# A fixed order of operations, and transposes by quarters, in a kernel of a recurrence and an MLP on one core

## The chip, the cores and the metric

One core of one Trainium2 chip. The time is the device time of one execution in microseconds (us); the span of a profile is some 1.7 us shorter than the time of its run. The engines are PE (TensorE; PEld is its weight load), DVE (VectorE), ACT (ScalarE), POOL (GpSimd) and SP (SyncE, which here only issues DMAs).

## The reference

```python
# r, k, v, w, a, b: 4 x 8 heads x 768 steps x 40, float32
for t in range(768):
    y[:, :, t] = einsum('bhd,bhde->bhe', rt, state)
    Sa = einsum('bhde,bhe->bhd', state, at)
    state = state * wt[:, :, None, :] - einsum('bhd,bhe->bhde', Sa, bt) \
          + einsum('bhd,bhe->bhde', vt, kt)
x = y as 3072 tokens x 320
g = softplus(x @ w_in)            # 320 -> 2048
out = g @ w_out                   # 2048 -> 320
```

The kernel does the recurrence in 12 chunks of 64 steps. For each pair of chunks ("window") it has to invert triangular blocks; the first two of the six inversions run on DVE and the last four on POOL. Around each chunk stand some 40 small groups of matmuls, among them six transposes of 128x1024 tiles (k, v, r, a, n, u), 72 in all.

## The kernel before

Every operation is an object with its reads, writes and engine. A greedy scheduler orders them at build time. It holds a model in which PE's instructions arrive in blocks of 256, and keeps slow operations (h, o, csb) for the places where a block ends. The constants are the model's own; the traces below show the 256, no run tests the others:

```python
BLOCK, AHEAD, FETCH, BEFORE = 256, 82, 2300.0, 70
SLOW = ("h", "o", "csb")
FILL, SAVE, MARGIN = 10826.01, 385707354.55, 0

class Fetch:
    def run(self, start, cost, n, keep=False):      # n: PE instructions of the operation
        ...                                         # cut: walks over the block borders
            if at == edge:
                w = max(0.0, asked + FETCH - t)     # the next block isn't there yet
                stall += w
                t += w
...
                if e == "pe":
                    pen += fetch.run(s + pen, c, 2 * COUNT[o.name])
                    if o.name in SLOW:
                        want = FILL if fetch.wants(s) else -SAVE
```

A transpose is 8 products over the whole array:

```python
        def transpose(src, srcs, t, off):
            def f(e):
                for bp in X2:
                    for yy in range(H_ // 2):
                        i = T.transpose(pb(t)[:, bp, off + 128 * yy:off + 128 * yy + 128],
                                        src[:, bp, 128 * yy:128 * yy + 128], ident[:, :])
                return i
            return op(pe(8 * 56.0), srcs + ["ident"], [t], f, mode=FULL, name="tr")
```

Line numbers in views of this kernel: L664 input loads, L705 sum over wout, L730 transposes, L773 grams, L967 and L971 POOL's inversion, L960 the transpose into mt that starts an inversion, L976 the mb product that ends it, L1205 and L1224 the two products of the MLP.

Of the kernel before, what the change touches and what calls it, by code (L numbers as in the profile page):

```python
# [15 lines left out]
L = 64  # L16
# [6 lines left out]
FIRST = ["v3", "b1", "v0", "w2", "k3", "b3", "b2", "r1", "k2", "v2", "r2", "b0", "a3", "v1", "a0", "a2", "k1", "k0",  # L23
    "w0", "a1", "r0", "r3"]
BY_ACT = ("a2", "b0", "k0h", "k3h", "r1h", "r2", "r2h", "v1", "w0",)
# [3 lines left out]
DUE = {}  # L29
TUNED = {("const", 0): (-3.417, 6.015), ("logs", 0): (8.233, 4724148.243), ("logs", 2): (6.841, 0.057),  # L30
    ("logs", 4): (27.193, 37726.657), ("logs", 6): (2.37, 391.709), ("logs", 8): (14.554, 0.031),
    ("logs", 10): (8.533, 0.075), ("first", 0): (-7.498, 4.706), ("first", 1): (-5.316, 0.851),
    ("first", 2): (7.047, 0.321), ("first", 3): (12.848, 2139.634), ("first", 4): (-17.941, 0.029),
    ("first", 5): (-5.232, 3.903), ("first", 6): (-2.842, 1.343), ("first", 7): (-9.63, 0.459),
    ("first", 8): (-0.391, 1.153), ("first", 9): (-12.18, 0.032), ("first", 10): (-3.891, 0.348),
    ("first", 11): (-5.631, 0.071), ("invert", 0): (-22.825, 124.863), ("invert", 1): (-5.682, 0.826),
    ("invert", 2): (-8.703, 0.205), ("invert", 3): (-3.704, 1.381), ("invert", 4): (-11.375, 1974.653),
    ("invert", 5): (-15.966, 18675.296), ("weights", 0): (11.186, 0.069), ("csb", 0): (19.338, 0.424),
    ("before", 0): (-9.639, 3.123), ("before", 1): (-0.307, 0.833), ("before", 2): (-7.054, 0.041),
    ("before", 3): (3.482, 0.394), ("before", 4): (-2.541, 0.33), ("before", 5): (-1.866, 0.119),  # L40
    ("before", 6): (-7.662, 6.411), ("before", 7): (7.568, 1.936), ("before", 8): (-2.958, 0.61),
    ("before", 9): (5.556, 0.241), ("before", 10): (3.509, 267110.005), ("before", 11): (-3.86, 15.709),
    ("W", 0): (14.734, 23.158), ("W", 1): (0.519, 1.563), ("W", 2): (2.341, 16.473),
    ("W", 3): (-3.294, 0.056), ("W", 4): (-1.178, 0.263), ("W", 5): (13.312, 49401.102),
    ("W", 6): (-3.378, 0.377), ("W", 7): (18.075, 0.091), ("W", 8): (6.58, 0.055), ("W", 9): (-16.669, 0.712),
    ("W", 10): (9.283, 52.11), ("W", 11): (5.588, 5.518), ("chain", 0): (-1.124, 0.658),
    ("chain", 1): (-1.317, 6.807), ("chain", 2): (-0.072, 0.086), ("chain", 3): (0.801, 0.66),
    ("chain", 4): (-0.995, 0.105), ("chain", 5): (-1.411, 10.836), ("chain", 6): (4.897, 11.085),
    ("chain", 7): (6.353, 307.324), ("chain", 8): (6.613, 11.615), ("chain", 9): (-7.081, 16.525),
    ("chain", 10): (0.443, 0.025), ("chain", 11): (-4.429, 7146.58), ("after", 0): (-0.303, 0.423),  # L50
    ("after", 1): (-8.387, 1.433), ("after", 2): (-1.682, 0.269), ("after", 3): (-16.392, 0.075),
    ("after", 4): (-13.518, 0.174), ("after", 5): (-11.687, 4.319), ("after", 6): (-6.304, 14.814),
    ("after", 7): (-11.267, 7.2), ("after", 8): (13.486, 10.526), ("after", 9): (0.785, 0.169),
    ("after", 10): (-1.398, 0.029), ("after", 11): (-8.768, 0.036), ("mlp", 0): (-8.041, 4.047),
    ("mlp", 1): (-5.331, 0.069), ("mlp", 2): (-5.684, 0.09), ("mlp", 3): (-6.455, 0.429),
    ("mlp", 4): (-9.333, 0.438), ("mlp", 5): (-15.828, 2.29), ("mlp", 6): (-18.549, 0.02),
    ("mlp", 7): (-5.284, 0.029), ("mlp", 8): (-11.139, 8.71), ("mlp", 9): (5.482, 16.833),
    ("mlp", 10): (-13.205, 18.475), ("mlp", 11): (-5.182, 0.355), ("load w", 4): (-6.939, 16.423),
    ("load w", 6): (-2.291, 0.065), ("load w", 8): (-4.5, 2.09), ("load w", 10): (-8.097, 83.127),
    ("load a", 4): (-1.093, 7.381), ("load a", 5): (12.999, 232.282), ("load a", 6): (-5.685, 150.299),  # L60
    ("load a", 7): (-6.287, 0.467), ("load a", 8): (8.128, 0.02), ("load a", 9): (21.502, 0.203),
    ("load a", 10): (-13.753, 0.788), ("load a", 11): (19.743, 62.662), ("load b", 4): (-5.978, 3.007),
    ("load b", 5): (-6.732, 26.773), ("load b", 6): (-15.345, 42671.34), ("load b", 7): (-9.402, 930.573),
    ("load b", 8): (-18.389, 1513.939), ("load b", 9): (-10.847, 80.591), ("load b", 10): (-14.935, 372.451),
    ("load b", 11): (-16.972, 2570.875), ("load k", 4): (-3.826, 10.505), ("load k", 5): (-15.524, 5807.389),
    ("load k", 6): (-6.188, 192.352), ("load k", 7): (-17.635, 719690.433), ("load k", 8): (-15.96, 2784.456),
    ("load k", 9): (-1.453, 375.087), ("load k", 10): (-22.642, 248.71), ("load k", 11): (-9.44, 14.74),
    ("load v", 4): (-10.722, 8957201.34), ("load v", 5): (5.402, 75.257), ("load v", 6): (11.64, 137128.864),
    ("load v", 7): (3.577, 7946.204), ("load v", 8): (1.82, 1286492.642), ("load v", 9): (11.637, 0.83),
    ("load v", 10): (-0.375, 23529.721), ("load v", 11): (0.874, 18043.764),  # L70
    ("load r", 4): (-12.216, 481.059), ("load r", 5): (-0.558, 0.561), ("load r", 6): (-2.182, 0.845),
    ("load r", 7): (-9.889, 580669.095), ("load r", 8): (-8.828, 15940.927),
    ("load r", 9): (-5.276, 1095633.975), ("load r", 10): (13.622, 714172.543), ("load r", 11): (5.476, 0.162)}
# [27 lines left out]
class Op:  # L101
    def __init__(self, engines, reads, writes, fn, mode=None, dma=None, name="", fence=None):
        self.engines = engines
        self.fence = fence
        self.fn = fn
        self.mode = mode
        self.dma = dma
        self.name = name
        self.preds = set()
        self.tiles = list(dict.fromkeys(t for t in map(tile_of, list(reads) + list(writes)) if t))  # L110
        self.tail = 0.0
        self.eng = None
        self.start = self.end = self.seen = 0.0


class Graph:


    def __init__(self):
        self.ops = []  # L120
        self.res = {}
        self.streams = {}
        self.tag = ""
        self.stage = (0.0, 0.0)
        self.stages = {}
        self.chunk = {}

    def op(self, engines, reads, writes, fn, mode=None, dma=None, name="", fence=None):
        o = Op(engines, reads, writes, fn, mode, dma, name, fence)
# [29 lines left out]
        self.stages.setdefault(self.tag, (self.stage, []))[1].append(o)  # L159
        return o  # L160

    def deadlines(self):

        for (due, length), ops in self.stages.values():
            for i, o in enumerate(ops):
                o.due = due + length * (i + 0.5) / len(ops)


LAT = {"pe": 240.0, "dve": 130.0, "act": 150.0, "pool": 130.0, "sp": 0.0}
SELF = 75.0  # L170
SWITCH = 150.0
PEN = 311.61
PERIOD = 25000.0
BETA = 0.67


BLOCK, AHEAD, FETCH, BEFORE = 256, 82, 2300.0, 70

PORT = ("scale", "fw")
SLOW = ("h", "o", "csb")  # L180
FILL, SAVE, MARGIN = 10826.01, 385707354.55, 0
COUNT = {"tr": 8, "tot": 16, "gram": 32, "cum": 8, "W": 32, "X1": 16, "X": 32, "D": 32, "U": 32,
         "S1": 4, "S": 64, "sT": 32, "y1": 16, "y": 64, "yT": 6, "h": 6, "o": 4, "csb": 16}


class Fetch:
    def __init__(self):
        self.at = BEFORE
        self.asked = 0.0
        self.total = 0.0  # L190

    def run(self, start, cost, n, keep=False):

        at, asked, left, t = self.at, self.asked, n, start
        stall = 0.0
        each = cost / n
        while left:
            edge = (at // BLOCK + 1) * BLOCK
            step = min(left, edge - at)
            ask = edge - AHEAD  # L200
            if at < ask <= at + step:
                asked = t + each * (ask - at)
            t += each * step
            at += step
            left -= step
            if at == edge:
                w = max(0.0, asked + FETCH - t)
                stall += w
                t += w
        if keep:  # L210
            self.at, self.asked = at, asked
            self.total += stall
        return stall
# [39 lines left out]
def schedule(ops):  # L253
# [18 lines left out]
    while ready:  # L272
        cands = []
        for o in ready:
# [22 lines left out]
            if not ok:  # L297
                continue
# [1004 lines left out]
```

## Time and profile before

The time is 348.28 us (348.22 to 350.63, 3 runs). The prediction below shows the page's busy shares and three stretches: A, to the third transpose into mt (112.7 us); B, the four inversions on POOL (181.6 us); C, the rest (51.5 us).

### The profile page before, as it was taken

To read this page: it belongs to the slowest core of one execution; us is meant where nothing else is said; L and a number is where in the kernel's file an instruction comes from. 1 tells how busy PE (TensorE), PEld (TensorE's weight loads), DVE (VectorE), ACT (ScalarE), POOL (GpSimd) and SP (SyncE) were. 2 spreads that over 40 slices of the span, in tenths; PEclk is the share of its full clock that TensorE was granted. 3 is DMA by queue.
4 is the path that set the end of the run, shared out by engine and by line. 5 is a ranking of instruction groups with operands and counts; after the bars stand their busy time and mean duration, and the time that the engine had idled before them with its cause. 6 is when DMAs were issued, how large, how long until landed. Compare 5 with 4: busy or idle time off the path is not lost.

```text
span 345.8 us, 17638 instructions
## 1 busy us (share of the span) xinstructions
PE 280.4 (81%) x8016; PEld 212.7 (61%) x8016; DVE 232.7 (67%) x419; ACT 210.3 (61%) x296; POOL 169.2 (49%) x309
## 2 busy tenths in 40 slices
PE   0337247688789969999799999998989899999873
PEld 0226126576567747777577776786766678777642
DVE  7729978889997746657756697585885656664201
ACT  1246704226797825877568888667687368667661
POOL 8106000001000627898888788898888888000000
PEclk9967865569999978999899999999999999999999
DMA  8999984687667565676546465430411400100101
GB/s 134 171 174 142 182 159 79 107 145 113 122 120 156 103 112 94 123 126 108 102 79 104 83 104 96 78 69 14 89 34 21 91 14 13 33 6 21 39 22 38
DMA packets 145787, 31.30 MB, mean 90 GB/s; under 512 B 140272, under 2 KB 145392, under 8 KB 145712
## 3 DMA queue, kind: packets, MB, share of 16 engines
q1 hardware_dynamic: 129504, 25.09, 42.9%
q10 hardware_dynamic: 13728, 2.46, 5.1%
q0 software_dynamic: 2480, 2.62, 4.7%
q8 instruction: 63, 1.03, 1.2%
q14 instruction: 12, 0.10, 0.1%
HBM read 28.84 MB, written 3.93 MB: 95 GB/s over the span
## 4 chain that ended last, share of the span: by engine, by line
PE 47%; ACT 11%; POOL 9%; DMA 9%; SPq 9%; DVE 7%; issue 5%; ACTq 2%; DVEq 0%; POOLq 0%
PE ps L1205 12%; PE ps L1224 12%; SPq L664 8%; PE ps L730 7%; POOL mt L971 4%; DMA wout<-in_moe_w_out_dram 3%; POOL mtmp L967 3%; ACT gT L1214 3%; ACT et L1211 3%; PE ps L773 2%; DMA a_f<-in_a_dram 2%; PE ps L1073 2%; ACTq L664 2%; DMA r_f<-in_r_dram 2%; PE ps L1174 2%
## 5 line engine op out<-in xcount | busy, mean ns | idle before, releaser
L1205 PE MATMUL ps<-xT,win 128*128 128x256 bf16 x576 | 79.9, 275 | 3.5 <-ACT et L1211 1.8
L1211 ACT ACTIVATE et<-ps 128x512 f32<-128x512 f32 x96 | 57.2, 596 | 36.3 <-PE ps L1205 35.8
L967 POOL TENSOR_TENSOR mtmp<-mt 128x30 f32<-128x30 f32 (+14 forms) x120 | 60.5, 504 | 33.0 <-DVE mt L960 24.3
L971 POOL TENSOR_TENSOR mt<-mt,mtmp 128x30 f32<-128x30 f32 (+14 forms) x120 | 66.8, 557 | 8.7
L1224 PE MATMUL ps<-wout,gT 128*128 128x320 bf16 x384 | 65.2, 302 | 5.9 <-ACT gT L1214 2.9
L1205 PEld LDWEIGHTS ps<-xT,win 128*128 128x128 bf16 x576 | 50.6, 98 | 15.9 <-ACT et L1211 6.0
L1214 ACT ACTIVATE gT<-et,hln 128x1024 bf16<-128x1024 f32 x48 | 55.2, 1151 | 1.4
L1224 PEld LDWEIGHTS ps<-wout,gT 128*128 128x128 bf16 x384 | 34.2, 98 | 20.1 <-ACT gT L1214 4.6
L1035 POOL CAST r_b<-r_f 128x640 bf16<-128x640 f32 x12 | 9.5, 789 | 44.2 <-DMA r_f<-in_r_dram 39.6
L1035 POOL CAST v_b<-v_f 128x640 bf16<-128x640 f32 x12 | 9.2, 765 | 37.0 <-DMA v_f<-in_v_dram 24.8
L1229 DVE TENSOR_TENSOR osb<-ps,csb 128x320 f32<-128x320 f32 x24 | 11.6, 484 | 20.3 <-PE ps L1224 20.1
L785 DVE TENSOR_TENSOR qt<-ps,sut 128x1024 bf16<-128x1024 f32 x12 | 14.6, 1221 | 5.6 <-PE ps L773 5.6
L814 PE MATMUL ps<-lw,nexc 64*64 64x320 bf16 x96 | 7.2, 361 | 13.8 <-ACT lw L845 13.6
L814 PE MATMUL ps<-lw,ninc 64*64 64x320 bf16 x96 | 9.8, 328 | 8.5 <-ACT ginv L862 6.2
L785 DVE TENSOR_TENSOR tak<-ps,sut 128x1024 bf16<-128x1024 f32 x12 | 14.6, 1219 | 2.8 <-PE ps L773 2.6
L785 DVE TENSOR_TENSOR pt<-ps,sut 128x1024 bf16<-128x1024 f32 x12 | 14.6, 1216 | 2.6 <-PE ps L773 2.6
L1180 DVE TENSOR_TENSOR yo<-ps,gexc 128x640 bf16<-128x640 f32 x12 | 9.9, 821 | 8.3 <-PE ps L1174 8.2
L845 ACT ACTIVATE lw<-w_f 128x1280 bf16<-128x1280 f32 x6 | 7.7, 1282 | 12.3 <-DMA w_f<-in_w_dram 12.3
L868 DVE TENSOR_TENSOR kh<-k_f,ginv 128x640 bf16<-128x640 f32 x12 | 10.9, 910 | 4.8 <-DMA k_f<-in_k_dram 4.8
L985 ACT ACTIVATE dex<-dc,blk 128x1024 bf16<-128x1024 bf16 x6 | 6.9, 1146 | 11.6 <-DVE dc L979 11.6
L866 DVE SCALAR_TENSOR_TENSOR nh<-b_f,ginv 128x640 bf16<-128x640 f32 x12 | 9.9, 825 | 5.3 <-ACT ginv L862 5.3
L862 ACT ACTIVATE ginv<-ps 128x640 f32<-128x640 f32 x12 | 8.4, 704 | 8.0 <-issue 6.8
(152 smaller groups left out, 587.9 us busy)
## 6 DMA issues: line engine op xcount, KB each, us to landing
out_dram<-osb SPq DMA_DIRECT2D x48, 80.0 KB, 2.3
b_f<-in_b_dram SPq DMA_DIRECT2D x44, 80.0 KB, 3.6
v_f<-in_v_dram SPq DMA_DIRECT2D x44, 80.0 KB, 3.3
a_f<-in_a_dram SPq DMA_DIRECT2D x44, 80.0 KB, 3.4
k_f<-in_k_dram SPq DMA_DIRECT2D x44, 80.0 KB, 3.6
r_f<-in_r_dram SPq DMA_DIRECT2D x42, 80.0 KB, 3.1
w_f<-in_w_dram SPq DMA_DIRECT2D x20, 160.0 KB, 4.2
wout<-in_moe_w_out_dram POOLq DMA_DIRECT2D x4, 320.0 KB, 10.0
```

The lines of the kernel that those rows point to most:

```text
L664: lambda e, bp=bp, x=x, q=q: queue(e).dma_start(heads(t[q:q + 64, bp, :], D_), SRC[n][2 * bp + x][:, c * L:(c + 1) * L, :].rearrange("h p ...
L730: i = T.transpose(pb(t)[:, bp, off + 128 * yy:off + 128 * yy + 128], src[:, bp, 128 * yy:128 * yy + 128], ident[:, :])
L785: lambda e: V.tensor_tensor(parity(dst), bh(pf(t), L), bc4(mask[:, :], L), ALU.mult), name="mask")
L814: i = T.matmul(pf(t)[s:s + 64, bp, 0:DM], mats[z][q:q + 64, :], heads(lwt[q:q + 64, bp, :], 2 * D_)[:, :, z * D_:z * D_ + D_], start=(z == ...
L967: lambda e, j=j, nt=nt, tv=tv: E_.tensor_tensor(tv, m[:, 0:j, j:j + 1].to_broadcast([128, j, nt]), m[:, j:j + 1, j + 1:32].to_broadcast([1 ...
L971: lambda e, j=j, tv=tv: E_.tensor_tensor(m[:, 0:j, j + 1:32], m[:, 0:j, j + 1:32], tv, ALU.add),
L1035: lambda e, dst=dst, src=src: P.tensor_copy(hd(dst), bh(src, D_)), name="cast")
L1205: i = T.matmul(one(t)[:, 256 * (q % 2):256 * (q % 2) + 256], win[:, z, q * 128:(q + 1) * 128], xT_[:, z, :], start=(z == 0), stop=(z == 2))
L1211: lambda e, q2=q2, t=t, ett=ett: A.activation(ett[:, q2 % 2, :], one(t), AF.Exp), name="exp")
L1214: lambda e, q2=q2, ett=ett: A.activation(gts[q2 // 2][0][:, :, :].rearrange("p q m -> p (q m)"), ett[:, :, :].rearrange("p q m -> p (q m)" ...
L1224: i = T.matmul(one(t)[:, 0:DM], gts[z][0][:, q % 4, bp * 128:(bp + 1) * 128], wout[:, q, :], start=(q == 0), stop=(q == NQ - 1))
L1229: lambda e, t=t, ot=ot: V.tensor_tensor(ot[:], one(t)[:, 0:DM], csb[:], ALU.add), name="oe")
```

## The change

The intent: an order of all 1,839 operations, drawn up ahead by a local search, replaces the scheduler, and with it the scheduler's model of blocks. ACT may issue every input load, and does issue 61 of them (26 before). Of the 72 transposes 55 go by 64x64 quarters, 32 products in place of 8. Some operations change their engine as well (by the pages ACT has 284 instructions in place of 296, POOL 318 in place of 309). The work is otherwise the same. The core of the diff:

```diff
-BLOCK, AHEAD, FETCH, BEFORE = 256, 82, 2300.0, 70
-class Fetch:
-    ...
-def schedule(ops):
-    ...
+ORDER = (105, 86, 0, 97, 64, 103, ...)        # 1,839 numbers
+ENGINE = ("ggggvvvv...")                      # an engine for each
+BANK = ("4244426664...")                      # a PSUM bank for each tile
+QUARTERS = (
+    "111011110111100111111110110111111011101110011111111110011110110111010110")
+def arrange(ops):
+    ...                                       # hands out banks, returns
+    return [ops[n] for n in ORDER]
 ...
-                        i = T.transpose(pb(t)[:, bp, off + 128 * yy:off + 128 * yy + 128],
-                                        src[:, bp, 128 * yy:128 * yy + 128], ident[:, :])
+                        n = off + 64 * (4 * bp + yy)
+                        for q in (0, 64) if mode == QUAD else ():
+                            for o in (0, 64):
+                                i = T.transpose(pb(t)[o:o + 64, q // 64, n:n + 64],
+                                                src[q:q + 64, bp, 128 * yy + o:128 * yy + o + 64], eye(q))
+                        if mode == FULL:
+                            i = T.transpose(...)          # as before
 ...
-                    op(issuers(n, c, bp), [], [nm + "%d%d" % (bp, x)],
+                    op({"sp": 680.0, "act": 680.0}, [], [nm + "%d%d" % (bp, x)],
 ...
-        g.deadlines()
-        order = schedule(g.ops)
+        order = arrange(g.ops)
```

Line numbers in views of the changed kernel: L560 loads, L629 transposes by quarters, L632 whole ones, L601 sum over wout, L722 running sums, L875 and L879 POOL's inversion, L868 transpose into mt, L1115 and L1134 the MLP.

## The prediction

> **What bounds the kernel now.** I read the page first (busy shares, then the slices), because a kernel with five engines at 49 to 81% has no single bound and one must see when each engine is full.
>
> ```profile
> PE 280.4 (81%) x8016; PEld 212.7 (61%) x8016; DVE 232.7 (67%) x419; ACT 210.3 (61%) x296; POOL 169.2 (49%) x309
> ...
> DVE  7729978889997746657756697585885656664201
> ...
> POOL 8106000001000627898888788898888888000000
> ```
>
> The DVE digits are 7 to 9 in the first third and fall afterwards; POOL is nearly empty up to slice 13, then 8 to 9 without a break up to slice 34, then nothing. So there are three stretches. The tile view of mt gives the two borders: the third transpose into mt (the start of the first inversion that POOL does) begins at 112.65 us, and the last mb product of POOL ends at 294.3. Busy times in these windows (columns: window, its length, then busy us and count for PE, PEld, DVE, ACT, POOL, then clock, DMA share, GB/s):
>
> ```profile
> 0.00:112.70 112.70, 69.62 (x1984) 52.21 (x1985) 91.66 (x213) 55.01 (x77) 18.88 (x45) 0.82 0.88 139
> 112.70:294.30 181.60, 168.20 (x5090) 129.78 (x5088) 122.68 (x177) 125.85 (x178) 150.28 (x264) 0.97 0.45 79
> 294.30:345.80 51.50, 42.59 (x947) 30.70 (x945) 18.36 (x30) 29.44 (x43) 0.05 (x1) 0.99 0.12 26
> ```
>
> Stretch A (112.7 us): DVE is busy 91.7, idle 21.0. DVE sets it, with the loads behind it (DMA share 0.88). Stretch B (181.6): POOL runs four inversions one after another, 264 instructions, busy 150.3; PE is busy 168.2. Both are close to the bound. Stretch C (51.5): the last two chunks and their MLP, PE 42.6.
> Next the waits and the timelines, for what the stretches lose:
>
> ```profile
> PE ps L705 <- DMA wout<-in_moe_w_out_dram: 5.6, 1, 5.6
> ...
> ACT ginv L862 <- issue: 6.8, 1, 6.8
> ...
> DVE nh L866 <- ACT ginv L862: 5.3, 1, 5.3
> ```
> ```profile
> 130.98 0.72 POOL L1035 CAST v_b<-v_f 128x640 bf16<-128x640 f32 x1 [7.49 <-DMA v_f<-in_v_dram]
> ```
>
> The ACT timeline shows what "issue" is: ACT is issuing six DMAs from 14.4 to 21.8 while ginv is due, and DVE waits behind it. In the chain from 112 to 126 there is nothing but SP issuing one load after another at 0.64 us each; v lands last, and POOL stands 7.5 us in the middle of its inversion.
>
> [...] These lines of the PE timeline (start, duration) let one read the rate from start to start:
>
> ```profile
> 182.47 0.61 PE L730 MATMUL ps<-ident,kh 128*128 128x128 bf16 x8
> 182.92 0.61 PE L730 MATMUL ps<-ident,v_b 128*128 128x128 bf16 x8
> 183.37 0.71 PE L1224 MATMUL ps<-wout,gT 128*128 128x320 bf16 x4
> ...
> 185.70 0.45 PE L773 MATMUL ps<-aT,kT 40*64 40x64 bf16 x32
> 185.98 0.45 PE L814 MATMUL ps<-lw,ninc 64*64 64x320 bf16 x4
> ...
> 189.39 0.61 PE L730 MATMUL ps<-ident,nh 128*128 128x128 bf16 x8
> 189.93 0.47 PE L814 MATMUL ps<-lw,nexc 64*64 64x320 bf16 x8
> ```
>
> A transpose by 8 whole blocks takes 0.45 us (182.47 to 182.92 to 183.37); 0.54 when a quarter-array operation follows (189.39 to 189.93). L1205 shows the same: 0.66 before a full-array operation, 0.76 before a quarter one. So a switch costs 0.10 us. Thirty-two 64x64 products on four quarters take 0.28 us (185.70 to 185.98).
> [...] 0.45/8 is 56 ns, [...] 0.28/32 is 8.8 ns, with four tiles at work.
> [...] The page has 63 packets of 1.03 MB on the instruction queue, and 16,032 PE instructions are 62.6 blocks. [...] PEld's idle time ended by "issue" adds up to some 20 us.
> [...] One queue at 0.64 us per 80 KB gives at most 125 GB/s, while the first slices reach 171 to 182. So here issue time matters.
>
> **The change, part by part.** I compared the order of instructions in the two built programs; no arithmetic is added or taken away, 8,016 matmuls become 9,336 only because 55 of 72 transposes now go by 32 quarters instead of 8 blocks.
> - Quarters: 55 x (0.45 - 0.28) = 9.4 us less PE work. That a 64x64 transpose runs as fast as a 64x64 product has a witness in the kernel before: L926 transposes dex by 32 such quarters, and the next group starts 0.28 us after it (96.29 to 96.57 in the PE timeline).
> - Mode switches: 243 before, 185 after; 58 x 0.10 = 5.8 us. Together 15 us of 251 us warm PE work (each kind of group by its start-to-start time, summed).
> - Cost: 2,640 more PE instructions, 10 more code blocks. At 20 us for 63 blocks that is 3 us if they are placed no better than now.
> - Loads: ACT issues 61 input loads instead of 26, SP 203 instead of 238, in another order. The weight loads stay with POOL. ACT's first exponents now stand before most of its issues, w goes first on both queues, and the sum over wout (L705, which held PE 5.6 us) moves from PE row 22 to row 40, behind the inversion products.
> - Order: before the third transpose into mt, DVE has 201 instructions instead of 213. Less: two rT, one vT, one aT copies (0.69 each), xb 0.44, dex 0.54, two osb 0.49, omask 0.64, eight memsets of about 0.2, in all 7.0. More: kT 0.69, kh 0.82, yb 0.44, two tlo 0.6, in all 3.2. So DVE work is 91.7 - 3.8 = 87.9. Both DVE inversions are interleaved now, so each fills the other's waits.
>
> Stretch A: 87.9 of DVE plus idle. Of the 21.0 us idle I take off the 5.3 behind ginv, 1.4 behind the wout sum, and 1 of the start: 13 left, A = 101.
> Stretch B: POOL has the same 264 instructions. 181.6 less the 7.5 wait is 174. PE has to do 159.5 us of warm work between the same two borders in the new order (158.7 in the old, where it took 181.6). That fits, but barely; I add 1: B = 175.
> Stretch C: 37.1 us of PE work after the last inversion against 40.0, by the same sums, so 3 less, and 2 less waiting: C = 46.5. The very end stays: the last MLP goes exp, ln, last products, sum, store, and ACT sets it.
> Sum 322.5 of span. The time is 1.8 (profiled run) to 2.5 us (medians) above the span: **324.5 us**, say 324. The parts on the path are A -12, B -7, C -5; the 15 us of PE work are mostly not a gain of their own in A and B, they are what allows DVE and POOL to run without waiting.
>
> **Rivals.**
> - POOL stays the bound and nothing before it moves: if the new A is no shorter, because DMA (share 0.88 in A) is the true limit, only B and C gain: 336. For it: 141 input loads stand before the third mt transpose, against 138. Against it: many of these aren't needed by then.
> - PE takes B over: with fetch stalls in runs of quarter operations (18,672 instructions, in B also 93% full) B ends at 180 instead of 175. Then 330.
> - ACT becomes the loser: 35 more issues of about 0.66 us are 23 us of ACT time, on top of 210 busy. ACT waited 36 us for L1205 alone, so there is room, but a DMA issue that stands before an exp or a copy on the chain delays the chain. It would cost some us in A; 328 to 332.
> - The search did better than I think: A near 95 (DVE 92% full), no waits in B, C at 43: 314.
> - The order was drawn up for durations that the chip doesn't keep; a fixed order then waits in place where it could have gone on. Since the old order was fixed at build time as well, this is no new weakness; I give it little.
>
> **Range and chances.** The rivals lie at 314 to 336 and I see none above 341.3 (2% faster) except two of them at once, or a new stall that the order cannot show. Range 313 to 336; faster 0.93, within 2% 0.05, slower 0.02.
>
> **What would show it.** Windows with the new borders: third mt transpose at 96 to 107, last mb end 173 to 178 later, rest 43 to 50. PE timeline: quarter transposes 0.28 us start to start. PE busy about 265. POOL without a wait above 3 us for v. The wait of L705 for wout gone, or off the chain. The prediction is wrong if the third mt transpose comes at 110 or later, if POOL stands waiting between inversions, or if the quarters take as long as the whole transposes (32 at over 14 ns) or "issue" before PE and PEld grows by over 8 us.

## More of the kernel before

```profile
q8 instruction: 63, 1.03, 1.2%
...
PE 47%; ACT 11%; POOL 9%; DMA 9%; SPq 9%; DVE 7%; issue 5%; ACTq 2%; DVEq 0%; POOLq 0%
...
POOL mtmp L967 <- DVE mt L960: 24.3, 1, 24.3
```

The reader is to see that 63 packets of instructions come, a number that looks harmless beside 1.2%; that POOL is part of the chain; and that POOL waits for mt once, before its first inversion, and never between two of them.

## The result, and the profile after

The changed kernel takes **366.92 us** (364.8 to 368.9, 4 runs), the kernel before in the same rounds 348.71 (348.22 to 350.63). The ratio is 1.0511, 95% interval 1.0439 to 1.0582: slower. A ratio is the mean time of one kernel's fast runs over that of the other's fast runs of the same rounds, so it isn't quite the ratio of the medians. Executions over 1.5% slower than the fastest of the same kernel are left out of the means.

The page after, busy times first, then the instruction queue and the chain:

```profile
PE 283.2 (78%) x9336; PEld 210.9 (58%) x9336; DVE 236.2 (65%) x422; ACT 200.9 (55%) x284; POOL 170.5 (47%) x318
...
q8 instruction: 73, 1.20, 1.3%
...
PE 56%; DVE 16%; SPq 8%; issue 7%; ACT 6%; DMA 5%; ACTq 0%; DVEq 0%
```

PE's busy time, which I expected near 265, has not fallen, POOL has left the chain, and PE's share of it has grown. The granted clock isn't what made it slower: its mean was 0.948 in this run and 0.924 in that of the kernel before. The three stretches with the same borders (window, length, then busy us and count of PE, PEld, DVE, ACT, POOL, then clock, DMA share, GB/s):

```profile
0.00:120.20 120.20, 65.94 (x2377) 49.83 (x2378) 86.40 (x200) 54.98 (x72) 20.84 (x53) 0.90 0.81 131
120.20:312.20 192.00, 172.84 (x5964) 129.56 (x5965) 128.82 (x187) 117.39 (x171) 148.89 (x264) 0.97 0.40 74
312.20:365.10 52.90, 44.38 (x1010) 31.55 (x998) 20.94 (x35) 28.58 (x41) 0.75 (x2) 1.00 0.13 29
```

A is 7.5 us longer, B 10.4, C 1.4. In B POOL does the same 264 instructions in about the same 149 us, but now it waits itself. The list of waits (engine line waited for: us in total, times, longest):

```profile
POOL mtmp L875 <- DVE mt L868: 17.9, 4, 9.0
PEld ps L629 <- issue: 16.7, 15, 5.3
...
PE ps L629 <- issue: 3.8, 5, 1.3
...
PEld ps L981 <- issue: 3.8, 15, 0.5
```

POOL waits four times for mt, so three times between inversions, which the prediction named as a sign of being wrong. And PE stands at "issue", that is, for nothing that the profile shows: all such waits sum to 16.3 us before products (4.1 in the kernel before) and 46.9 before weight loads (20.7). The PE timeline shows how they look (start, duration, in brackets the idle time and what ended it):

```profile
92.80 1.46 PE L1115 MATMUL ps<-xT,win 128*128 128x256 bf16 x6
94.19 0.64 PE L629 MATMUL ps<-ident,ah 64*64 64x64 bf16 x32
94.64 0.24 PE L629 MATMUL ps<-ident,kh 64*64 64x64 bf16 x3
96.02 0.59 PE L629 MATMUL ps<-ident,kh 64*64 64x64 bf16 x29 [1.14 <-issue]
```

One transpose of 32 products stops after its third product for 1.14 us and goes on. No operand changes there, no semaphore is asked. Counting PE's instructions in the built program (a product is two, its weight load and itself; a second wait is one more) puts this stop, and the others like it, at number 192 modulo 256 in both kernels. I call the 256 instructions from one such place to the next a block: the queue's packets have 16,384 bytes each, and 73 of them came for 9,336 products (18,672 instructions are 72.9 times 256), 63 for 8,016 (62.6). At these stops a packet on the instruction queue starts 2.2 to 2.8 us before PE goes on (here at 93.69, 2.3 us before 96.02). I summed the time that PE loses at these borders (distance between the starts of two successive products, less the first product's own time, wherever a border lies between them and it is over 0.1 us). A recount from the traces alone, with less exact borders, gives 7.0 and 19.5 us for the two kernels, so a few us in these sums carry no weight:

| | PE lost at block borders, us | stops over 0.35 us |
|---|---|---|
| before | 6.6 | 7 |
| after | 23.3 | 28 |

By stretch it is 1.9, 4.4 and 0.2 before, and 5.5, 16.1 and 1.7 after. B's loss at borders grew by 11.7 us and B by 10.4. That the two are alike doesn't make the one the cause of the other; after_whole, below, shows that most of B's 10.4 us stays without the quarters.

### The profile page after: what moved, and what is told of

Read it like the earlier page. It is cut to its first block, busy times and chain, and to the rows that moved or that the text cites. A ratio compares the mean times of both kernels' runs of the same rounds, so it can differ in the third digit from the quotient of the medians.

```text
span 365.1 us, 20308 instructions
## 1 busy us (share of the span) xinstructions
PE 283.2 (78%) x9336; PEld 210.9 (58%) x9336; DVE 236.2 (65%) x422; ACT 200.9 (55%) x284; POOL 170.5 (47%) x318
## 4 chain that ended last, share of the span: by engine, by line
PE 56%; DVE 16%; SPq 8%; issue 7%; ACT 6%; DMA 5%; ACTq 0%; DVEq 0%
PE ps L1115 15%; PE ps L1134 11%; SPq L560 6%; PE ps L629 4%; PE ps L681 4%; ACT et L1121 3%; PE ps L1082 2%; PE ps L981 2%; PE ps L722 2%; PE ps L1041 2%; DVE tak L693 2%; PE ps L1015 2%; PE ps L1058 2%; PE ps L632 2%; DMA b_f<-in_b_dram 2%
## 5 line engine op out<-in xcount | busy, mean ns | idle before, releaser
L1115 PE MATMUL ps<-xT,win 128*128 128x256 bf16 x576 | 84.0, 284 | 3.6 <-issue 1.3
L875 POOL TENSOR_TENSOR mtmp<-mt 128x30 f32<-128x30 f32 (+14 forms) x120 | 61.3, 511 | 26.6 <-DVE mt L868 17.9
L879 POOL TENSOR_TENSOR mt<-mt,mtmp 128x30 f32<-128x30 f32 (+14 forms) x120 | 64.8, 540 | 8.6
L1134 PE MATMUL ps<-wout,gT 128*128 128x320 bf16 x384 | 65.9, 307 | 1.5 <-DVE osb L1141 1.4
L1115 PEld LDWEIGHTS ps<-xT,win 128*128 128x128 bf16 x576 | 51.9, 101 | 16.6 <-ACT et L1121 5.9
L1134 PEld LDWEIGHTS ps<-wout,gT 128*128 128x128 bf16 x384 | 35.8, 100 | 15.5 <-DVE osb L1141 2.5
L722 PE MATMUL ps<-lw,ninc 64*64 64x320 bf16 x96 | 13.1, 412 | 18.4 <-DVE ntot L493 12.0
L1141 DVE TENSOR_TENSOR osb<-ps,csb 128x320 f32<-128x320 f32 x24 | 11.6, 484 | 20.7 <-PE ps L1134 13.9
L1049 DVE TENSOR_TENSOR state<-ps,gtot 128x320 bf16<-128x320 f32 x22 | 10.4, 485 | 13.3 <-PE ps L1041 13.2
L722 PEld LDWEIGHTS ps<-lw,ninc 64*64 64x64 bf16 x96 | 6.2, 140 | 21.6 <-DVE ntot L493 12.0
L693 DVE TENSOR_TENSOR qt<-ps,sut 128x1024 bf16<-128x1024 f32 x12 | 14.7, 1222 | 6.0 <-PE ps L681 5.5
L1088 DVE TENSOR_TENSOR yo<-ps,gexc 128x640 bf16<-128x640 f32 x12 | 9.9, 824 | 12.6 <-PE ps L1082 11.4
L693 DVE TENSOR_TENSOR pt<-ps,sut 128x1024 bf16<-128x1024 f32 x12 | 14.6, 1217 | 0.6 <-PE ps L681 0.6
L693 DVE TENSOR_TENSOR tak<-ps,sut 128x1024 bf16<-128x1024 f32 x12 | 14.6, 1216 | 0.5 <-PE ps L681 0.5
L768 ACT ACTIVATE gexc<-ps 128x640 f32<-128x640 f32 x12 | 8.4, 702 | 10.9 <-DVE yo L1088 6.7
L789 ACT ACTIVATE mc<-ps,blk 128x512 f32<-128x512 f32 x12 | 8.2, 688 | 10.0 <-PE ps L681 9.9
L772 DVE TENSOR_TENSOR ah<-a_f,gexc 128x640 bf16<-128x640 f32 x12 | 11.3, 941 | 3.6 <-DMA a_f<-in_a_dram 3.1
```

Of the source, the lines that this page charges most:

```text
L693: lambda e: V.tensor_tensor(parity(dst), bh(pf(t), L), bc4(mask[:, :], L), ALU.mult), name="mask")
L722: i = T.matmul(pf(t)[s:s + 64, bp, 0:DM], mats[z][q:q + 64, :], heads(lwt[q:q + 64, bp, :], 2 * D_)[:, :, z * D_:z * D_ + D_], start=(z == ...
L875: lambda e, j=j, nt=nt, tv=tv: E_.tensor_tensor(tv, m[:, 0:j, j:j + 1].to_broadcast([128, j, nt]), m[:, j:j + 1, j + 1:32].to_broadcast([1 ...
L879: lambda e, j=j, tv=tv: E_.tensor_tensor(m[:, 0:j, j + 1:32], m[:, 0:j, j + 1:32], tv, ALU.add),
L1115: i = T.matmul(one(t)[:, 256 * (q % 2):256 * (q % 2) + 256], win[:, z, q * 128:(q + 1) * 128], xT_[:, z, :], start=(z == 0), stop=(z == 2))
L1134: i = T.matmul(one(t)[:, 0:DM], gts[z][0][:, q % 4, bp * 128:(bp + 1) * 128], wout[:, q, :], start=(q == 0), stop=(q == NQ - 1))
```

## The experiments

Theory **R** (rate): blocks come at a limited rate, so instructions that do little work cost more than their own time. Its rivals: **P** (place): only where a border falls counts; **O**: the order itself waits in the wrong places; **L**: the loads moved to ACT come late. Twelve kernels ran. All gave the right result.

| run | median us | runs | ratio to before | 95% interval | lost at borders, us |
|---|---|---|---|---|---|
| changed kernel | 366.92 | 4 | 1.0511 | 1.0439 to 1.0582 | 23.3 |
| after_whole | 357.14 | 4 | 1.0235 | 1.0168 to 1.0301 | 10.1 |
| before_quarters | 370.39 | 4 | 1.0616 | 1.0550 to 1.0683 | 37.5 |
| after_sp_loads | 374.09 | 4 | 1.0726 | 1.0643 to 1.0808 | 21.4 |
| after_fill128 | 369.87 | 4 | 1.0617 | 1.0535 to 1.0698 | 24.3 |
| before_fill128 | 359.97 | 4 | 1.0223 | 1.0165 to 1.0281 | 15.3 |
| search_whole (one of the 4 slow) | 342.62 | 4 | 0.9809 | 0.9746 to 0.9872 | 6.8 |
| search_nofetch | 361.22 | 4 | 1.0366 | 1.0309 to 1.0424 | 12.6 |
| after_search | 347.97 | 4 | 0.9875 | 0.9802 to 0.9948 | 6.8 |
| search_again (one of the 4 slow) | 344.40 | 4 | 0.9733 | 0.9665 to 0.9801 | 4.9 |

The last column is from the profiled run, so of one execution. Medians are of all runs, ratios of fast ones. The kernel before had 349.83, 349.38 and 351.23 us as medians in the three rounds of experiments, in which the runs from after_whole to after_sp_loads, then after_fill128, search_whole and search_nofetch, and then the others stood together.

### after_whole: the order kept, the quarters undone

```diff
-QUARTERS = ("1110111101111001111111101101...")
+QUARTERS = "000000000000000000000000000000..."
```

> The changed kernel with every transpose whole again; order, engines and banks kept. Theories: R (rate: TensorE's instructions arrive in blocks of 256, a block at best every 3.3 us, the smallest distance between two instruction packets in both traces; the quarters fill a block with too little work), P (place: what counts is whether a block's border falls into slow products; the order was drawn up around the borders), O (the order itself waits in the wrong places), L (the loads now issued by ACT come late). R: 2,640 fewer instructions, 10 blocks less, stalls at block borders fall from about 23 us to about 8, against 15 us more work of TensorE that lies partly in stalls: 350 to 360 us. P: every border moves to where nobody placed it, so stalls stay or grow and the 15 us of work come on top: 375 or more. O and L: nothing mended, up to 15 us more work: 367 to 380.

357.14 us, inside R's range and far from the others'. The profile has 63 instruction packets again. PE has more work of its own, and the kernel is 9.8 us faster than the changed one: **the quarters alone cost some 10 us where I counted a gain.** Of the 15 us of PE work that I counted as saved, 9.4 are the quarters'; of the 58 mode switches saved (from a full-array operation to a quarter one or back) they account for 16 only (the traces have 243 before, 185 after, 201 here), the order for the rest. Stretch A falls by 4.9 us (third transpose into mt at 115.34 instead of 120.21). It also shows that the quarters are not everything: 2.4% remain over the kernel before. They remain in B above all, which falls by 2.9 us only (in a profiled run that was the slowest of the four, 1.8 us above their median). PE's waits for "issue" in B fall from 11.3 us to 5.1, but POOL goes on waiting for mt:

```profile
115.30:304.40 189.10, 171.45 (x5067) 131.66 (x5066) 130.22 (x186) 115.71 (x169) 150.91 (x264) 0.97 0.40 74
...
POOL mtmp L874 <- DVE mt L867: 14.6, 3, 8.2
```

### before_quarters: the old order, with the quarters

```diff
-                        i = T.transpose(pb(t)[:, bp, off + 128 * yy:off + 128 * yy + 128], ...
+                        for q in (0, 64) if quarters else ():       # the same 55 of 72
+                            for o in (0, 64):
+                                i = T.transpose(pb(t)[o:o + 64, q // 64, n:n + 64], ...
```

> The kernel before in its own order, with the same 55 of 72 transposes by quarters, nothing else. R: 10 blocks more, stalls at borders rise from about 7 us to about 20, against 15 us less work: 345 to 356 us, so no gain from quarters. P: borders unplaced, 365 or more. O and L: the quarters as my prediction had them, a gain: 335 to 342.

370.39 us, 20.6 more than the kernel before, worse than R said and in P's range. PE's waits of that run, of transposes (L746 by quarters) and grams (L793):

```profile
PEld ps L746 <- issue: 12.1, 20, 2.5
PEld ps L793 <- issue: 10.3, 20, 1.5
PE ps L746 <- issue: 7.6, 6, 2.4
```

The loss at borders is 37.5 us, nearly twice what R expected. Here both bear on it: ten more blocks, and an order that was drawn for borders that lay elsewhere. O and L, for which the quarters were a gain, are out as the only cause; what the order adds is left to after_whole and the searches.

### after_shift128, after_fill128, before_fill128: only the borders moved

The first try repeats the first product 64 times, which moves every later border by 128 instructions:

```diff
+    fill.n = SHIFT            # 64: the next product is issued so many more times
     for o in order:
```

> The changed kernel with 64 filler products (128 instructions) ahead of the first product, which takes 0.6 us and moves every later block border by half a block; nothing else. R: the mean work in a block is the same, within 4 us of the changed kernel, 364 to 371. P: borders now fall into runs of small products: [...] 385 or more. O and L: 366 to 368.

385.45 us (six runs, three of them slow; the fast ones took 379.56 to 384.75), which looks like P. It isn't: the filler itself stands on the path.

```profile
11.66 16.71 PE L299 MATMUL ps<-lw,ninc 64*64 64x320 bf16 x62 [11.66 <-DVE nexc L506]
```

I had counted 0.6 us for 64 products of 320 columns; in a row they took 16.7, 0.27 us each. The first transpose into mt came at 45.6 us instead of 32.0. The run says nothing on P. The filler was then made of 64 products of 8 columns on a tile of zeros, in the first microseconds, in which PE has no data (in the view above it waits 11.66 us for its first):

```diff
+                for _ in range(64):
+                    i = T.matmul(psf[0:8, 0, 0:8], tiny[0:64, :], tiny[0:64, :])
-        emit(nc, st, order)
+        emit(nc, st, fill + order)
```

> The shift by half a block again, mended: the filler of the first try was 62 products of 0.26 us each in a row and took 16.7 us by itself. Now 64 products of 8 columns, on a small tile of zeros, in the first 12 us in which TensorE waits for data anyway. A replay (every operation in its own engine's order with its duration as recorded, every wait with the latency recorded, a new block of 256 TensorE instructions at the earliest 3.8 us after the block before was entered) gives 348, 362, 354, 367 and 371 us for the kernel before, the changed one, its whole-transpose form, the old order with quarters, and the one with loads on SyncE; measured were 346, 365, 357, 368 and 372 in the profiled runs. R (rate): the replay has 0.5 us for the shift, so 363 to 371. P (place of borders): 385 or more.

369.87 us. The first transpose into mt is at 32.01 us, as without it, so the filler costs nothing. P's 385 is refuted: in the changed kernel moving all borders by half a block is worth some 1%, which isn't clear of noise (the intervals of the two ratios overlap). The same on the kernel before:

> The kernel before with 64 tiny products in the idle first microseconds, so that each of its block borders moves by half a block. Its scheduler keeps a count of the blocks and holds slow products back for the borders. R: the replay has no change (347.9 to 348.0 us): within 4 us of the kernel before. P: 15 us or more slower.

359.97 us, 8.7 more than its partner, with 15.3 us lost at borders instead of 6.6. This lies between R and P: in the old order, whose scheduler keeps slow products for the borders, the place is worth 8.7 us. So **both count**: with fewer instructions less was lost (10.1 us at borders in after_whole, 23.3 in the changed kernel), and the old scheduler's placing had saved a good part of it. One shift of the borders was tried in each kernel, no other.

### after_sp_loads: the loads back to SP

```diff
-        o.eng = names[ENGINE[n]]
+        o.eng = "sp" if "sp" in o.engines else names[ENGINE[n]]
```

> The changed kernel with all 61 input loads that ACT issues given back to SyncE, at the same place in the order; every other engine's order is kept. L: the first stretch (to the third transpose into mt, 119.7 us now) shrinks by 5 us or more, 355 to 361 us. R, P and O: no gain, 364 to 372, since SyncE is no freer and issues one load every 0.65 us or so.

374.09 us, 7.2 slower than the changed kernel; the first transpose into mt moves from 32.0 to 38.3 us. L is refuted: in this order, 61 loads on ACT are some 7 us better than none. The kernel before had 26 on ACT already; what the step from 26 to 61 is worth was not run by itself.

### before_burst: the disputed cost by itself

```diff
+            for kind in ("quarters", "whole", "tiny"):     # after all other work
+                b = Op({"pe": 1.0}, [], [], lambda e, kind=kind: f(kind), mode=QUAD, name=kind)
+                b.preds.update(o for o in order if not o.dma)
```

> The disputed cost by itself. The kernel before, and after all its work TensorE does 24 transposes by quarters (768 products), then 24 whole ones (192 products), then 512 products of 8 columns, in one bank pair that nobody reads; nothing else runs. R: 1,536 instructions of quarters are 6 blocks and take at least 6 times 3.3 us, 20 to 23 us, that is 0.83 to 0.95 us a transpose, with a stop at every block; 384 instructions of whole transposes are 1.5 blocks and take their own 10.8 us, 0.45 each; 1,024 instructions of tiny products are 4 blocks, 13 to 15 us. My prediction: quarters 24 times 0.28, 6.7 us; whole 10.8 us; tiny products 4 us or less.

393.0 us with the added work. Its PE timeline:

```profile
345.30 2.47 PE L1287 MATMUL ps<-ident,nh 64*64 64x64 bf16 x238 [0.58 <-DVE osb L1229]
349.91 1.24 PE L1287 MATMUL ps<-ident,nh 64*64 64x64 bf16 x128 [2.15 <-issue]
353.38 1.92 PE L1287 MATMUL ps<-ident,nh 64*64 64x64 bf16 x128 [2.23 <-issue]
356.86 1.93 PE L1287 MATMUL ps<-ident,nh 64*64 64x64 bf16 x128 [1.55 <-issue]
360.33 1.92 PE L1287 MATMUL ps<-ident,nh 64*64 64x64 bf16 x128 [1.55 <-issue]
364.07 0.47 PE L1287 MATMUL ps<-ident,nh 64*64 64x64 bf16 x18 [1.82 <-issue]
364.48 12.89 PE L1281 MATMUL ps<-ident,nh 128*128 128x128 bf16 x192
377.30 7.69 PE L1278 MATMUL ps<-ident 64*8 64x8 bf16 x302
385.32 5.66 PE L1278 MATMUL ps<-ident 64*8 64x8 bf16 x210 [0.33 <-issue]
```

This shows the cost by itself, if in one execution. The first 238 products ran without a stop; from then on exactly 128 products, 256 instructions, came at a time, and the starts are 3.47, 3.48, 3.47 and 3.74 us apart (349.91, 353.38, 356.86, 360.33, 364.07), with nothing else at work but the last stores. The view gives the 128 products 1.24 us in the first of these groups and 1.92 or 1.93 in the next three (by my reading of the trace the granted clock fell to about half at some 352 us; the run's mean was 0.893); the distance stayed the same. **A block of instructions took about 3.5 us here, however little it did.** (The smallest distance between two packets of the instruction queue is 3.29 us in the changed kernel, 3.33 in the one before.) The queue has one packet between every two of these starts, at 351.05, 354.55, 357.91 and 361.38: it began 1.1 us after PE had entered a block, and PE went on 2.3 to 2.7 us after it began. Twenty-four transposes by quarters took 19.2 us, 0.80 each, a little under R's 20 to 23, the first 238 products having run without a stop; 24 whole ones 12.8 us, 0.53 each (0.45 at a granted clock of 1.00, in the prediction), without a stop. The tiny products, all on one place of the array, ran at 25 ns each (7.69 us for 302; on four quarters in turn it is 8.8 ns in the prediction's 0.28 us for 32), which fills a block in 3.2 us, and stopped only briefly (0.33 us). My 0.28 us for a transpose by quarters is the time inside a block; its 64 instructions are a quarter of a block, 0.87 us of supply at 3.47 us a block.

### Five searched orders

To ask what an order can do, I replayed the recorded run of a kernel: every operation in its engine's order, with its recorded duration and latencies, and a rule that a block is there at the earliest 3.8 us after the one before was entered. 3.8 is fitted, not measured: with it the replay gives 348, 362, 354, 367 and 371 us for the kernel before, the changed one, after_whole, before_quarters and after_sp_loads, whose profiled runs took 346, 365, 357, 368 and 372. A search over millions of moves of single operations within it gave new orders; engines, banks and the loads' place among themselves are kept.

```diff
-        order = schedule(g.ops)
+        schedule(g.ops)
+        order = [g.ops[n] for n in ORDER]
```

> The kernel before, whole transposes, engines and banks kept; only the order of operations on TensorE, VectorE, ScalarE and GpSimd is changed, by 24 million trial moves in the replay, which charges a block of instructions with 3.5 to 4.1 us. R: the replay says 324 us at 3.8 us a block (348 for the kernel before), nearly no stall at borders; since the chip won't keep every duration, 325 to 340. O (orders drawn from recorded durations are not kept by the chip): no gain, 345 to 360.

342.62 us, 1.9% faster than the kernel before, outside R's range by 2.6 us. O, as this expectation has it (the chip doesn't keep orders drawn from recorded durations), is refuted.

> The same search on whole transposes with a free instruction supply (0 us a block). It ends at 323 us by its own count, a little ahead of search_whole. R: with 3.8 us a block its order takes 345 us in the replay, 23 us of them stalls: 338 to 355 on the chip, so a search blind to the blocks loses nearly all that it counts on. If blocks don't matter to an order: as fast as search_whole.

361.22 us, 3.7% slower than the kernel before. By its own count this order was a little ahead of search_whole; on the chip it is 18.6 us behind, and 6 us above R's range. **This search, blind to the blocks, lost more than it found**, even with whole transposes. It is one order, and of the 18.6 us only 5.8 show as more lost at borders (12.6 against 6.8); where the rest goes was not traced. (How the changed kernel's own search counted blocks isn't to be seen: its file keeps the number of products, 32, beside a quartered transpose's cost, but not the model.)

> The same search from the old order with the 55 transposes by quarters (368 to 372 us unsearched). R: the replay says 341 us, 17 us of them stalls at borders; quarters stay behind whole transposes by 10 us or more even when the order is searched with the blocks in view: 338 to 356. If quarters are good in themselves and only the order was wrong: equal to search_whole or faster.

Inconclusive in its size: of four runs one counted as fast, 357.29 us; the other three, called slow, took 363.26 to 365.91. The fast run lies 14.7 us behind search_whole, as R has it, though 1.3 us above R's range; the same search with quarters did not reach search_whole.

> The changed kernel with whole transposes (357 us) and its order searched again in the replay with 3.5 to 4.1 us a block, loads where the changed kernel has them. The replay says 324 us at 3.8 us a block, against 354 for its starting point; search_whole came out 15 us above its replay. R: 332 to 345, so an explicit order pays once it is drawn with the blocks in view and without quarters. O: an explicit order as such waits in the wrong places: 352 to 362.

347.97 us, 9 us faster than after_whole by the medians of different rounds (3.6% by the ratios), from the same loads and engines; POOL's waits for mt fall from 14.6 us to 2.5, and B from 189.1 us to 177.8, while A, 116.8, is no shorter. R's range is missed by 3 us, O's by 4. So the fixed order's share of the loss can be mended by moving operations alone, for the most part in B.

> A second round of the search, from search_whole's order with the durations of its own trace. The replay says 328 us (332 for search_whole, which took 339 in the profiled run): R: 333 to 342 us. If the remaining distance between replay and chip is noise that no order can use: 341 to 346.

344.40 us where the kernel before took 351.23: ratio 0.9733, **the fastest of all against its own rounds**, though its interval overlaps that of search_whole. R's range (333 to 342) is missed; the time lies in the other one (341 to 346), for which what remains between replay and chip is noise that no order can use. Its stretches:

```profile
0.00:115.70 115.70, 73.70 (x1985) 54.53 (x1986) 90.65 (x212) 55.12 (x76) 18.43 (x45) 0.78 0.87 135
115.70:291.70 176.00, 165.92 (x5104) 126.90 (x5104) 121.70 (x178) 124.36 (x179) 152.18 (x264) 1.00 0.47 81
291.70:343.90 52.20, 44.03 (x930) 31.40 (x928) 19.42 (x31) 30.52 (x44) 0.64 (x1) 1.00 0.12 28
```

B takes 176.0 us against 181.6 before and 192.0 after: this is the stretch B that I had predicted (175), reached with whole transposes. A is no shorter than before. In the searches R's replay was too hopeful: the spans of the profiled fast runs of search_whole, search_nofetch, after_search and search_again are 15 to 21 us longer than it said. What it misses I did not find out.

## Why the prediction was wrong, point by point

**Quarters and their fetch cost.** The step that failed is the term "10 more code blocks ... that is 3 us if they are placed no better than now". I averaged 20 us of idle time of PEld over 63 blocks. Both halves are wrong: of those 20 us only 6.6 were lost by PE at borders, and what a block cost in the burst wasn't an average but a least time, 3.47 us. At that rate ten blocks more are 36 us more of supply (2,640 / 256 x 3.47). My own numbers could have shown it: 251 us of work in 62.6 blocks are 4.0 us a block, 236 in 72.9 are 3.2, and 3.2 lies below the 3.47 that a block took in the burst. For B alone, 5,964 products are 46.6 blocks and at the same rate 162 us of supply, beside the 175 that I predicted, and work isn't spread evenly over blocks. Measured: 16.7 us more lost at borders.

**"Thirty-two 64x64 products take 0.28 us", 9.4 us saved; 58 fewer switches, 5.8 us.** The 0.28 is right as the time inside a block (94.19 to 94.64 above at a granted clock of 0.50, and 0.25 to 0.28 at 1.00, where no stop falls into it and a quarter operation follows), wrong as a gain. The 58 switches are right as a count; no run tests the gain. A group before a switch took some 0.10 us longer (medians from start to start at a granted clock of 1.00: whole transposes of the kernel before 0.45 us before a full-array operation, 0.55 before a quarter one; groups of six products of the MLP's first half 0.665 and 0.76 in both kernels); 5.8 us for 58 was my estimate. A witness of one transpose between slow operations says nothing on many of them: 0.80 in a row.

**Stretch A: 101.** It took 120.2. The DVE work was right (87.9 predicted, 86.4 measured); the idle time was 33.8 us instead of 13. The waits that I took off did go (those for ACT fell from 7.4 to 3.6 us), and others came in their place: for PE 15.9 us instead of 7.7, for DMAs 7.1 instead of 0.9. The longest of DVE in A:

```profile
DVE kh L776 <- DMA k_f<-in_k_dram: 4.0, 1, 4.0
DVE gT L845 <- PE ps L842: 3.3, 1, 3.3
DVE ah L772 <- DMA a_f<-in_a_dram: 3.1, 2, 2.8
DVE ub L450 <- PE ps L1015: 2.7, 2, 2.2
```

The second of these sits behind PE's own stop at a border, in the group of 32 products of L842:

```profile
78.28 0.32 PE L842 MATMUL ps<-dex,gT 64*64 64x64 bf16 x16 [1.14 <-ACT uT L450]
80.14 0.32 PE L842 MATMUL ps<-dex,gT 64*64 64x64 bf16 x16 [1.54 <-issue]
```

DVE, idle for 33.8 us of A, is not its bound; a chain through PE, DVE and ACT in turn is likely, but not shown. Of the 7.5 us that A grew, 4.9 go with the quarters (after_whole) and the rest stays with the order. In no version did A get shorter than 112.6 us, though the second transpose into mt came as early as 51 us. What sets A's length is not settled: no run isolates it. The prediction's own rival, that the loads are the true limit, is open too: the DMA share in A was 0.88 before and 0.81 after, 0.87 in after_whole and 0.89 in search_whole, where A was 112.6.

**Stretch B: 175, "that fits, but barely; I add 1".** It took 192.0. The wait of 7.5 us for v fell to 3.5, but POOL stood 17.1 us for mt between its inversions, where it had not waited before. The term that failed is the 1 us that I added for PE not keeping up. The rival that PE takes B over by fetch stalls, sized at 5 us, is right in part: without the quarters B is 2.9 us shorter. The other 7.5 of its 10.4 us stay in after_whole, with 14.6 us of POOL's waits for mt, and go when the operations are put in another order (after_search, B 177.8). So in B, by these profiled runs, the order was the larger error. How much of it is borders is open.

**Stretch C: 46.5.** It took 52.9, with 1.7 us lost at borders; I did not look into the rest.

**"The order was drawn up for durations that the chip doesn't keep ... I give it little."** This was the second error: the old order was fixed at build time too, but with the blocks in its model. The new one, with whole transposes, is 2.4% slower than the old; reordering alone takes 9 us off it. That the chip doesn't keep the durations wasn't shown to be the reason. How much of that is borders and how much are other waits was not separated: 10.1 us were lost at borders against 6.6 in the kernel before.

**ACT as loser.** Not so: with its 61 issues on SP the kernel is some 7 us slower.

**The signs.** Three of those that I named for being wrong came true: the third transpose into mt at 120.21, POOL waiting between inversions, "issue" before PE and PEld up by 38 us. (PEld's part of this is no measure of loss: search_again, the fastest against its own rounds, has 36.7 us of it; PE's is 2.8 there, 4.1 before and 16.3 after.) Two small misreadings carry no weight: from 14.39 to 21.82 ACT issued seven loads, not six, and the chain from 112 to 126 has two stores among SP's loads. The range 313 to 336 and the chance of 0.93 left out one thing that the kernel before had in plain sight: a scheduler with a model of instruction blocks, which the change takes out.

## What to carry to other kernels

Count a change in TensorE instructions as well as in time: in the burst, with two instructions for each product, blocks of 256 that held less work than 3.47 us came at that distance all the same, 27 ns a product (3.47 / 128), and 24 transposes by few large products took 12.8 us, by many small ones 19.2. A duration read between slow neighbours isn't the cost in a row (0.28 and 0.80 us here); burst the operation at the end of the kernel and read the starts. An order searched in a model can lose what the model leaves out, as search_nofetch did; replay a recorded run of the old and of the changed kernel before you trust it, and expect the replay to be hopeful (15 to 21 us here).
